# Score products of 8 to 136 columns run on to 192 and 256 columns in a two-attention kernel

## The chip, the cores and the metric

One core of one Trainium2 chip runs the whole program. The metric is device time in microseconds (us): the median of repeated executions of a kernel. A separate execution is taken with the hardware profiler; everything that is read below from the page or the trace comes from that one.

## The reference

Two attention layers read inputs of their own, each 2048 positions by 1024 features with 32 heads of 32 features, and their outputs are set side by side:

```python
q, k, v = split(x @ wqkv)                      # both layers, 32 heads of 32
# layer A: query s sees keys s, s-2, ..., s-14 (8 keys, every second one)
# layer B: query s sees keys s-255 ... s
o = softmax(mask(q @ k.T * 32 ** -0.5)) @ v
y = o @ wo
return concatenate([yA, yB], axis=-1)
```

## The kernel before

**Tiling.** The work is cut into eight units of 512 positions: units 0 to 3 are layer B ("dense": each 128 queries meet up to 384 keys), units 4 to 7 are layer A ("window"). For layer A even and odd positions are first parted on the host, so that eight neighbouring keys are seen; each 128 queries then meet 136 keys. A unit that has keys ahead of its first position reads them as a halo (`has_halo`). Every unit has eight groups of four heads.

**Stages of a group.** Q and K are made by 48 TensorE products of 512 columns (line 418), written out in two parts, and stacked by DMA into the tiles `qst` (128 by 4 heads by 512) and `kst` (128 by 4 heads by 768), two buffers each. Then come two passes over the scores:

- The *first pass* (`first`, line 714) has a block of 128 queries as the stationary operand and n keys as the moving one; 16 products a group, n being 136 (window), 384 (dense), or 128 and 256 where a unit has no halo. VectorE masks each and takes the maximum (line 719), ScalarE takes the exponential and its sum (line 724). The 16 sums give one row of numbers for each head, which VectorE writes into rows 96 to 127 of `qst` (lines 753 and 759), head after head.
- The *second pass* (`second`, line 599 in `window`, line 799 in the dense case) has 128 keys as the stationary operand and n queries as the moving one, so that its result comes out transposed and already normalized after one exponential (lines 606 and 806). Here n is 8, 136 or 128 in the window units, and 128, 256 or 384 in the dense ones; two or four heads (`pack`) share a PSUM bank `ps`, at columns `i * n`. Masks follow on VectorE or GpSimd (lines 616, 612, 785, 788), and products with V (lines 640 and 846).

All scores are products of `fp32r` tiles, one matmul and one weight load each. The products with V read plain `f32` tiles and take two matmuls each. V itself is made on line 481 (256 or 512 columns), the output product is line 543 (512 columns); weights and x are split in two parts by VectorE (lines 164 and 172). Line 138 issues the loads of the weights.

**Order.** One loop writes the program out, with a model of the engines' times (`Clock`). It holds four lists: `aux` (line 753), second-pass items with the V products, first-pass items, and the big products of 512 or 256 columns. At each step it takes the item that the model says can begin first, so products of few columns stand between big ones. An item's cost in the model is a number given by hand. Scores go through a ring of four PSUM banks (`rs`, `NS` = 4), and a bank is taken again when ScalarE's exponential has read it.

Of the kernel before, what the change touches and what calls it, by code (L numbers as in the profile page):

```python
# [14 lines left out]
P = 128  # L15
# [14 lines left out]
NX, NST, NN = 9, 1, 3  # L30
TAIL, XAT = 4, 1
C1, C3, CG, CV = 0.108, 0.2, 0.231, 0.242
TERMS = ((0, 0), (0, 1), (1, 0))


# [146 lines left out]
def kernel(ctx, tc, xs, wqk, wv, wo, outs, units):  # L182


    nc = tc.nc
    U = len(units)
    ctx.enter_context(tc.manual_schedule())
    const = ctx.enter_context(tc.tile_pool(name="const", bufs=1))
    raws = ctx.enter_context(tc.tile_pool(name="raws", bufs=NRAW))
# [41 lines left out]
    for p in plan:  # L231
# [3 lines left out]
        elif p[0] == "v":  # L235
            s0, n = VPARTS[p[2]]
# [102 lines left out]
    def qk_items(u, s):  # L339
# [58 lines left out]
        for t in range(2):  # L398
# [14 lines left out]
            def run(k, t=t, h=h):  # L413
                if k == 0:
                    h["ps"], h["b"] = rg.take()
                    h["w"], _ = st.get(where["qk", u, s, t])
                for i, (a, b) in enumerate(TERMS):
                    nc.tensor.matmul(h["ps"], h["w"][:, a, k * P:(k + 1) * P], xt[u][k][:, b, :],  # L418
# [101 lines left out]
    def o_items(u, n):  # L520
        h = {}

        last = u == U - 1
        ring = rs if last and n == 3 else rg

        def ready(k):
            if (u * NG + k) not in done["ot"]:
                return None
            if k == 0:
                st.split_to(where["o", u, n] + 1)  # L530
                r = st.ready[where["o", u, n]]
                h["r"] = r if isinstance(r, list) else [r, r]
                return latest(ring.when(), h["r"][0], done["ot"][u * NG])
            return max(done["ot"][u * NG + k], h["r"][k // 4])

        def run(k):
            if k == 0:
                h["ps"], h["b"] = ring.take()
                w, _ = st.get(where["o", u, n])
                h["w"] = [(w[i // 4], i % 4 * P) if isinstance(w, list) else (w, i * P) for i in range(NK)]  # L540
            w, c = h["w"][k]
            for i, (a, b) in enumerate(TERMS):
                nc.tensor.matmul(h["ps"], w[:, a, c:c + P], ot[u, k][:, b, :],  # L543
                                 start=(k == 0 and i == 0), stop=(k == NK - 1 and i == 2))
            if k == 3 and (not last or n == 0 or n > 2):
                st.split_to(where["o", u, n] + (3 if last and n == 0 else 2))
            if k == 5 and last and n in (1, 2):
                st.split_to(where["o", u, n] + 3)

        def after(k):  # L550
            if k == NK - 1:
                done["out"][u, n] = True
                for f in list(stores.values()):
                    f()
                o = pbuf[:, n % 4, :S] if last else stp.tile([P, S], F32, tag="ost", name="ost")
                e = copy_out(o, h["ps"], h["b"], ring)

                def store():
                    if stores.pop((u, n), None):
                        nc.scalar.dma_start(outs[u, n], o)  # L560
                        ck.load("store", e)

                stores[u, n] = store
                ck.defer(e, store)

        return [(lambda k=k: ready(k), lambda k=k: run(k), 3 * CG, lambda k=k: after(k)) for k in range(NK)]

    def x_items(u):
        xt[u], xready[u] = [], []

        def run(g):
            a, b = st.get(where["x", u, g])
            xt[u] += a
            xready[u] += b

        return [[(lambda: 0.0, lambda g=g: run(g), 0.0, lambda: None)] for g in range(4)]


    def window(u, s, h):
        has_halo = units[u][3]  # L580
        buf = s % 2
        hg = u * NG + s
        q, kk = qst[buf], kst[buf]
        vp, vc = vpart[s]
        v = vbuf[vp]
        two = []
        kbs = [(-1, 0, 8, 4)] if has_halo else []
        kbs += [(0, 0, 136, 2), (1, 128, 136, 2), (2, 256, 136, 2), (3, 384, 128, 4)]
        nk = len(kbs)
        at = [sum(k[2] for k in kbs[:i]) for i in range(nk)]  # L590

        def second(ki, hp):
            kb, q0, n, pack = kbs[ki]
            if hp == 0:
                h["left", ki] = 4 // pack
            ps, bank = rs.take()
            for i in range(pack):
                j = hp * pack + i
                nc.tensor.matmul(ps[:, i * n:(i + 1) * n], kk[:, j, 256 + kb * P:256 + (kb + 1) * P],  # L599
                                 q[:, j, q0:q0 + n], start=True, stop=True)  # L600
            w = pbuf[:, hp * pack:hp * pack + pack, at[ki]:at[ki] + n]
            if ki == nk - 1 and hp == 4 // pack - 1:
                free_keys(hg)

            def expo():
                nc.scalar.activation(w, ps[:, :pack * n].rearrange("p (j n) -> p j n", j=pack), AF.Exp)
                e = ck.use("act", pack * n / 1200 + 0.055, ck.now, pfree[0])
                rs.give(bank, e)

                def masks():  # L610
                    if kb < 0:
                        nc.gpsimd.affine_select(w, w, pattern=[[0, pack], [-1, n]], compare_op=ALU.is_ge, fill=0.0,
                                                base=-121, channel_multiplier=1)
                        r = ck.use("pool", 0.21, e)
                    else:
                        nc.vector.tensor_tensor(w, w, cst["keep_w"][:, None, :n].to_broadcast([P, pack, n]),  # L616
                                                op=ALU.min)
                        r = ck.use("dve", pack * n / 960 + 0.07, e, port=True)
                    h["left", ki] -= 1
                    h["pr", ki] = max(h.get(("pr", ki), 0.0), r)  # L620

                ck.defer(e - 0.1, masks)

            return expo

        def values_ready(ks):
            if ks[-1] == nk - 1 and hg >= NO and ((hg - NO) // NG, NG - 1) not in done["out"]:
                return None
            if (u, vp) not in done["v"] or any(h.get(("left", k), 1) for k in ks):
                return None  # L630
            return latest(done["v"][u, vp], ro.when() if ks[0] == 0 else 0.0, *[h["pr", k] for k in ks])

        def values(ks):
            for ki in ks:
                kb, q0, n, pack = kbs[ki]
                if ki == 0:
                    h["o"], _ = ro.take()
                slot = (4 * u + kb) % 6
                for j in range(4):
                    nc.tensor.matmul(h["o"][32 * j:32 * j + 32, q0:q0 + n],  # L640
                                     v[:, slot, vc + 32 * j:vc + 32 * j + 32], pbuf[:, j, at[ki]:at[ki] + n],
                                     start=(ki == 0), stop=(ki == nk - 1), skip_group_check=True)

            def after():
                pfree[0] = ck.now
                finish(u, s, h)

            return after

        def seconds(ki):  # L650
            pack = kbs[ki][3]
            for hp in range(4 // pack):
                two.append(Item(lambda hp=hp: latest(rs.when(), h["rows"] and h["rows"][hp * pack + pack - 1]),
                                lambda ki=ki, hp=hp: second(ki, hp), pack * C1))

        for ki in range(nk):
            seconds(ki)
        ks = tuple(range(nk))
        two.append(Item(lambda: values_ready(ks), lambda: values(ks), C3 + sum(max(0.05, kbs[k][2] / 592) for k in ks)))
        return two  # L660
# [28 lines left out]
    def attention(u, s):  # L689
# [3 lines left out]
        q, kk = qst[buf], kst[buf]  # L693
# [5 lines left out]
        def first(b, j):  # L699
# [6 lines left out]
            else:  # L706
                full, mask = 136, cst["mask_w"]
                cut = 8 if (b == 0 and not has_halo) else 0
            n = full - cut
            c1 = 256 + P * b + P  # L710
            c0 = c1 - n
            i = j * 4 + b
            ps, bank = rs.take()
            nc.tensor.matmul(ps[:, :n], q[0:96, j, b * P:(b + 1) * P], kk[0:96, j, c0:c1],  # L714
                             start=True, stop=True)
            nm, sm = h["nm"][:, i:i + 1], h["sm"][:, i:i + 1]

            def top():
# [72 lines left out]
        def second(ki, hp):  # L791
            kb, q0, n, pack = kbs[ki]
# [3 lines left out]
                h["left", ki, pr] = 2 // pack  # L796
            ps, bank = rs.take()
            for i, j in enumerate(heads):
                nc.tensor.matmul(ps[:, i * n:(i + 1) * n], kk[:, j, 256 + kb * P:256 + (kb + 1) * P],  # L799
                                 q[:, j, q0:q0 + n], start=True, stop=True)  # L800
            w = pbuf[:, heads[0]:heads[0] + pack, at[ki]:at[ki] + n]
            if ki == nk - 1 and hp == 4 // pack - 1:
                free_keys(hg)
# [66 lines left out]
    for u in range(U):  # L870
        for s in range(NG):
            a, b = attention(u, s)
# [21 lines left out]
    n = TAIL  # L894
# [84 lines left out]
```

## Time and profile before

| | |
|---|---|
| median of 3 runs | 1926.64 us (1926.56 to 1929.82) |
| profiled execution: its time, its span | 1927.66 us, 1926.0 us |
| TensorE matmul (PE) busy | 1897.7 us, 99% of the span |
| weight loads (PEld) busy | 1565.1 us, 81% |
| VectorE (DVE), ScalarE (ACT), GpSimd (POOL) busy | 74%, 50%, 20% |
| mean granted TensorE clock | 0.997 |
| products of line 714 / 599 / 799 | 1024 / 576 / 704 |

PE is matmul work, PEld the loads of the stationary operand. A group row of the profile gives the line, the operation, the tiles written and read, rows times columns of the stationary operand, the moving operand and the count, then busy time, the mean duration of one in ns, and the engine's idle time ahead of them with what ended it. A duration holds the way through the array, so that durations of neighbours overlap; what a product costs a busy TensorE is read from the times at which stretches of products begin.

### The profile page before, as it was taken

The page shows a single profiled execution, that of the slowest core. Times are in us where ns is not written, and L with a number is a line of the kernel's source. Part 1 is how long each engine was busy: PE and PEld are TensorE (multiplying, and loading weights), DVE is VectorE, ACT ScalarE, POOL GpSimd, SP SyncE. Part 2 cuts the span into 40 slices and gives each one's busy share as a digit, 9 for nine tenths or more (in the row PEclk, how much of TensorE's full clock was granted, in tenths as well). Part 3 has the DMA queues.
Part 4 walks back from the last instruction along what each step waited for, and adds up shares of the span by engine and source line. Part 5 has one row for each costly group of instructions (what it writes and reads, how often), then busy time and mean ns, then how long its engine had stood idle before and what let it go on. Part 6 is the DMA issues. An engine that isn't in the chain of part 4 may idle for free. (4 is left out here: it accounts for less than half of the span.)

```text
span 1926.0 us, 34516 instructions
## 1 busy us (share of the span) xinstructions
PE 1897.7 (99%) x11840; PEld 1565.1 (81%) x11840; DVE 1430.3 (74%) x3989; ACT 965.1 (50%) x3139; POOL 385.7 (20%) x926
## 2 busy tenths in 40 slices
PE   8999999999999999999999999999999999999999
PEld 6887687888778887788877888888888888888887
DVE  6777767669777688777787778866796768867673
ACT  3565665655665656664565434533444444534451
POOL 2223432323221322222322001100010000100000
PEclk9999999999999999999999999999999999999999
DMA  6555545455545455545464556456564655555451
GB/s 191 153 143 159 164 146 167 138 152 174 156 144 171 121 164 152 156 143 151 132 165 129 163 171 193 131 167 180 141 184 141 176 163 176 153 167 167 128 149 66
DMA packets 135727, 297.96 MB, mean 155 GB/s; under 512 B 14464, under 2 KB 40064, under 8 KB 135552
## 3 DMA queue, kind: packets, MB, share of 16 engines
q1 hardware_dynamic: 83456, 123.77, 26.1%
q0 software_dynamic: 41472, 151.01, 23.7%
q10 hardware_dynamic: 10624, 20.98, 3.0%
q8 instruction: 94, 1.54, 0.4%
q14 instruction: 81, 0.66, 0.1%
HBM read 167.77 MB, written 27.26 MB: 101 GB/s over the span
## 5 line engine op out<-in xcount | busy, mean ns | idle before, releaser
L418 PE MATMUL g<-x,w 128*128 128x512 f32 x3072 | 798.2, 397 | 8.8 <-DVE w L164 8.2
L418 PEld LDWEIGHTS g<-x,w 128*128 128x128 f32 x3072 | 555.5, 189 | 106.6 <-DVE w L164 8.6
L724 ACT ACTIVATE s<-s,nm 128x384 f32<-128x384 f32 (+3 forms) x1024 | 452.7, 443 | 224.1 <-DVE nm L719 214.6
L481 PE MATMUL g<-w,x 128*128 128x256 f32 (+1 forms) x2304 | 404.6, 322 | 0.9 <-DVE w L172 0.7
L543 PE MATMUL g<-ot,w 128*128 128x512 f32 x1416 | 356.8, 398 | 0.0
L481 PEld LDWEIGHTS g<-w,x 128*128 128x128 f32 x2304 | 332.5, 190 | 26.6 <-DVE w L172 2.5
L172 DVE TENSOR_TENSOR w<-raw,w 128x512 fp32r<-128x512 f32 x518 | 339.7, 697 | 8.9
L719 DVE CUSTOM_DVE_ANT_0 s<-s,mask_d 128x384 f32<-128x384 f32 (+2 forms) x512 | 263.0, 554 | 93.4 <-PE s L714 92.3
L543 PEld LDWEIGHTS g<-ot,w 128*128 128x128 f32 x1416 | 259.6, 190 | 50.8 <-issue 1.0
L785 POOL TENSOR_SCALAR_AFFINE_SELECT pbuf<-pbuf 128x128 f32<-128x128 f32 (+1 forms) x600 | 213.8, 384 | 313.0 <-ACT pbuf L806 303.0
L806 ACT ACTIVATE pbuf<-s 128x384 f32<-128x384 f32 (+2 forms) x480 | 202.8, 503 | 94.2 <-PE s L799 93.3
L714 PE MATMUL s<-kst,qst 96*128 96x384 f32 (+3 forms) x1024 | 238.0, 302 | 5.6 <-ACT s L724 4.4
L714 PEld LDWEIGHTS s<-kst,qst 96*128 96x128 f32 x1024 | 182.5, 189 | 51.8 <-ACT s L724 10.8
L719 DVE CUSTOM_DVE_ANT_0 s<-s,mask_w 128x136 f32<-128x136 f32 (+1 forms) x512 | 141.9, 323 | 103.4 <-PE s L714 102.4
L724 ACT ACTIVATION_READ_ACCUMULATOR s<-s,nm 128x1 f32 x1024 | 210.4, 206 | 0.0
L355 ACT ACTIVATE nat<-g 128x512 fp32r<-128x512 f32 x128 | 76.6, 599 | 240.2 <-PE g L418 225.6
L759 DVE TENSOR_TENSOR qst<-s,pick 32x512 fp32r<-32x512 f32 x256 | 158.4, 675 | 37.9 <-PE s L753 37.0
L164 DVE CAST w<-raw 128x1024 fp32r<-128x1024 f32 x259 | 179.3, 692 | 7.0 <-DMA raw<-wv 4.0
L359 DVE SCALAR_TENSOR_TENSOR nat<-g,nat 128x512 fp32r<-128x512 f32 x128 | 88.3, 690 | 116.1 <-ACT nat L355 115.5
L138 POOL DMA_DIRECT2D raw<-wqk x126 | 68.7, 545 | 496.6 <-DVE w L172 234.7
L799 PEld LDWEIGHTS s<-qst,kst 128*128 128x128 f32 x704 | 112.8, 189 | 42.6 <-ACT s L724 14.9
L719 DVE DVE_READ_ACCUMULATOR2_ANT nm<- 128x1 f32 x1024 | 144.4, 141 | 0.5
(55 smaller groups left out, 1184.8 us busy)
## 6 DMA issues: line engine op xcount, KB each, us to landing
raw<-wqk POOLq DMA_DIRECT2D x126, 512.0 KB, 3.9
qst<-nat SPq DMA_DIRECT2D x192, 256.0 KB, 3.8
kst<-nat SPq DMA_DIRECT2D x192, 256.0 KB, 4.0
raw<-wv POOLq DMA_DIRECT2D x70, 512.0 KB, 4.4
raw<-wo POOLq DMA_DIRECT2D x64, 512.0 KB, 4.0
raw<-xs POOLq DMA_DIRECT2D x28, 512.0 KB, 4.6
outs<-ost ACTq DMA_DIRECT2D x56, 256.0 KB, 2.6
halo<-nat SPq DMA_DIRECT2D x40, 256.0 KB, 4.4
```

The lines of the kernel that those rows point to most:

```text
L164: nc.vector.tensor_copy(t[:, 0, :], raw)
L172: nc.vector.tensor_tensor(o, a, b, op=ALU.subtract)
L418: nc.tensor.matmul(h["ps"], h["w"][:, a, k * P:(k + 1) * P], xt[u][k][:, b, :], start=(k == 0 and i == 0), stop=(k == NK - 1 and i == 2))
L481: nc.tensor.matmul(ps, xt[u][kw * g + k][:, a, p0:p0 + P], h["w"][g][:, c, k], start=(first and t == 0 and half == 0), stop=(last and t == 2),
L543: nc.tensor.matmul(h["ps"], w[:, a, c:c + P], ot[u, k][:, b, :], start=(k == 0 and i == 0), stop=(k == NK - 1 and i == 2))
L714: nc.tensor.matmul(ps[:, :n], q[0:96, j, b * P:(b + 1) * P], kk[0:96, j, c0:c1], start=True, stop=True)
L719: nc.vector.tensor_tensor_reduce(ps[:, :n], ps[:, :n], mask[:, cut:full], scale=-1.0, scalar=BIG, op0=ALU.add, op1=ALU.min, accum_out=nm)
L724: nc.scalar.activation(ps[:, :n], ps[:, :n], AF.Exp, bias=nm, scale=-1.0, accum_out=sm)
L759: nc.vector.tensor_tensor(q[96:P, j, :].rearrange("p (b s) -> p b s", s=P), ps[0:32, None, 0:P].to_broadcast([32, 4, P]), cst["pick"][0:32 ...
L785: nc.gpsimd.affine_select(w, w, pattern=[[0, m], [step, n]], compare_op=ALU.is_ge, fill=0.0, base=base, channel_multiplier=chan)
L799: nc.tensor.matmul(ps[:, i * n:(i + 1) * n], kk[:, j, 256 + kb * P:256 + (kb + 1) * P], q[:, j, q0:q0 + n], start=True, stop=True)
L806: nc.scalar.activation(w, ps[:, :pack * n].rearrange("p (j n) -> p j n", j=pack), AF.Exp)
```

## The change

A helper `wide` widens the products of the second pass: up to 256 moving columns, as far as the bank (`512 - c`) and the four heads' queries (`2048 - 512 * j - q0`) go. The added columns are the queries that follow in `qst`, which can be the next head's. They land in PSUM columns that the next head's product of the same bank overwrites, or that nobody reads. First-pass products are widened to 192 keys: for the first block of queries to the right, for the others to the left, and VectorE and ScalarE then read the n columns that count. Products that already have as many columns stay as they are. `ORDER` is the order 0 to 7 that the units had. The costs in the ordering model are not changed, nor is any operation on another engine.

By the loops, 544 first-pass products go to 192 columns (448 from 136, 96 from 128). Of the second pass, 736 go to 256 columns: 384 from 136, 288 from 128 and 64 from 8; 64 products of 128 columns stay, since the fourth head has no columns behind it.

```diff
+ORDER = (0, 1, 2, 3, 4, 5, 6, 7)
+WIDE1, WIDE2 = 192, 256
...
+    units, xs = [units[i] for i in ORDER], [xs[i] for i in ORDER]
...
-                        nc.scalar.dma_start(outs[u, n], o)
+                        nc.scalar.dma_start(outs[ORDER[u], n], o)
...
+    def wide(ps, c, n, keys, q, j, q0):
+        x = max(n, min(WIDE2, 512 - c, 2048 - 512 * j - q0))
+        nc.tensor.matmul(ps[:, c:c + x], keys, q.rearrange("p j s -> p (j s)")[:, 512 * j + q0:512 * j + q0 + x],
+                         start=True, stop=True)
...
 # second, in window and in the dense case
-                nc.tensor.matmul(ps[:, i * n:(i + 1) * n], kk[:, j, 256 + kb * P:256 + (kb + 1) * P],
-                                 q[:, j, q0:q0 + n], start=True, stop=True)
+                wide(ps, i * n, n, kk[:, j, 256 + kb * P:256 + (kb + 1) * P], q, j, q0)
...
 # first
-            nc.tensor.matmul(ps[:, :n], q[0:96, j, b * P:(b + 1) * P], kk[0:96, j, c0:c1],
-                             start=True, stop=True)
+            x = max(n, WIDE1)
+            if b == 0:
+                nc.tensor.matmul(ps[:, :x], q[0:96, j, :P], kk[0:96, j, c0:c0 + x], start=True, stop=True)
+            else:
+                nc.tensor.matmul(ps[:, :x], q[0:96, j, b * P:(b + 1) * P], kk[0:96, j, c1 - x:c1], start=True, stop=True)
+                ps = ps[:, x - n:]
```

More of the change, by code (lines that the diff above doesn't have):

```diff
@@ L798, in second @@
             for i, j in enumerate(heads):
-                nc.tensor.matmul(ps[:, i * n:(i + 1) * n], kk[:, j, 256 + kb * P:256 + (kb + 1) * P],
-                                 q[:, j, q0:q0 + n], start=True, stop=True)
+                wide(ps, i * n, n, kk[:, j, 256 + kb * P:256 + (kb + 1) * P], q, j, q0)
             w = pbuf[:, heads[0]:heads[0] + pack, at[ki]:at[ki] + n]
```

## The prediction

> **What bounds the kernel now.** I read the page's busy line first, then the groups kept apart by shape, then the timeline of TensorE around products of few columns, and last the windows of the tail.
>
> ```profile
> PE 1897.7 (99%) x11840; PEld 1565.1 (81%) x11840; DVE 1430.3 (74%) x3989; ACT 965.1 (50%) x3139; POOL 385.7 (20%) x926
> ```
>
> TensorE is busy for 1897.7 of 1926.0 us. Whatever a product costs more there goes to the end, unless it falls ahead of a place where TensorE would have waited anyway. So the question is what a product of few columns costs now, and what one of 192 or 256 costs. The groups give counts and durations:
>
> ```profile
> L714 PE MATMUL s<-kst,qst 96*128 96x136 f32 x448 | 83.1, 261 | 4.1 <-ACT s L724 3.9
> L714 PE MATMUL s<-kst,qst 96*128 96x256 f32 x32 | 7.8, 304 | 0.0
> L599 PE MATMUL s<-qst,kst 128*128 128x136 f32 x384 | 53.5, 273 | 0.1
> L599 PE MATMUL s<-qst,kst 128*128 128x8 f32 x64 | 8.3, 235 | 0.0
> L799 PE MATMUL s<-qst,kst 128*128 128x256 f32 x224 | 41.0, 289 | 0.2 <-ACT s L724 0.2
> L799 PE MATMUL s<-qst,kst 128*128 128x128 f32 x224 | 35.8, 258 | 2.0 <-ACT s L724 1.8 <-DVE qst L759 0.2
> ```
>
> Durations overlap, so they are no price on a full engine. The price is in the timeline (first column the start, second the length, last the count): the time from one stretch's start to the next one's, shared among its products.
>
> ```profile
> 1242.25 2.69 PE L418 MATMUL g<-x,w 128*128 128x512 f32 x11
> 1244.77 1.72 PE L599 MATMUL s<-qst,kst 128*128 128x8 f32 x14
> 1246.32 0.90 PE L418 MATMUL g<-x,w 128*128 128x512 f32 x3
> ...
> 1865.49 0.90 PE L543 MATMUL g<-ot,w 128*128 128x512 f32 x3
> 1866.23 1.27 PE L599 MATMUL s<-qst,kst 128*128 128x136 f32 x10
> 1867.33 0.90 PE L543 MATMUL g<-ot,w 128*128 128x512 f32 x3
> 1868.08 0.56 PE L599 MATMUL s<-qst,kst 128*128 128x128 f32 x4
> 1868.47 0.50 PE L714 MATMUL s<-kst,qst 96*128 96x136 f32 x3
> 1868.81 0.91 PE L543 MATMUL g<-ot,w 128*128 128x512 f32 x3
> ...
> 399.76 3.04 PE L481 MATMUL g<-w,x 128*128 128x256 f32 x24
> 402.64 0.33 PE L799 MATMUL s<-qst,kst 128*128 128x128 f32 x2
> ...
> 285.04 0.86 PE L418 MATMUL g<-x,w 128*128 128x512 f32 x3
> 285.74 0.64 PE L799 MATMUL s<-qst,kst 128*128 128x256 f32 x4
> 286.21 1.55 PE L418 MATMUL g<-x,w 128*128 128x512 f32 x6
> ```
>
> - 512 columns: 11 products from 1242.25 to 1244.77, 0.229 us each; I use 0.23.
> - 136 columns: from 1865.49 to 1867.33 lie three of 512 and ten of 136; (1.84 - 0.69) / 10 = 0.115 us.
> - 128 columns, and first-pass ones of 136: from 1867.33 to 1868.81 lie three of 512, four of 128 and three of 136; (1.48 - 0.69) / 7 = 0.113 us. I take 0.112 for 128.
> - 8 columns: the stretch at 1244.77 holds ten of 136 and four of 8 (the row names its first shape); 1.55 / 14 = 0.111 us.
> - 256 columns: 24 from 399.76 to 402.64, 0.120 us each; from 285.04 to 286.21 three of 512 and four of 256: (1.17 - 0.69) / 4 = 0.120 us.
>
> The reader is to see that 8, 128 and 136 columns cost the same 0.111 to 0.115 us. Something other than columns sets that price; each product has one load of 128 stationary columns, and I take that load to be it. From 256 to 512 columns the price rises by 0.11 us, 0.43 ns a column; back from 256 on that slope, columns set the price only above some 240.
>
> **The change part by part.** Nothing is removed. No instruction, wait, transfer or order changes as written; what changes is the length of 1280 products.
>
> *First pass, 544 products to 192 columns.* By the slope 192 columns take 120 - 64 x 0.43 = 92 ns, under the 111 to 115 ns that the load takes. Price: 0 on a full TensorE, hidden by the loads. If that cover is gone, because the engine stands free when the product comes, its end counts: on the durations of 96 rows (261 at 136, 304 at 256) 192 columns end some 20 ns later, 544 x 20 = 10.9 us if all of them counted. A gain has no row to come from: the loads remain. I take 0, since TensorE is 99% busy.
>
> *Second pass, 736 products to 256 columns.* 384 x (120 - 115) = 1.9 us; 288 x (120 - 112) = 2.3 us; 64 x (120 - 111) = 0.6 us; together 4.8 us, all on TensorE. From below: if 256 columns cost no more than the floor of 112 ns, 0 for those of 128 and 384 x 3 = 1.2 us gained on those of 136, so -1 us. From above, by the ends of products (289 ns against 273, 258 and 235): 384 x 16 + 288 x 31 + 64 x 54 = 18.5 us. I take 4.8: the row of 24 in a stretch is the nearest to a full engine.
>
> *What swallows some of it.* The list of TensorE's waits has ten of up to 1.6 us on VectorE or ScalarE (five of line 714 for line 724, five of line 753 for line 745). Products added shortly before such a place run while VectorE works on. With 20 us ahead of each of ten places, 200 of 1926 us, a tenth is swallowed: an estimate, 0.5 us.
>
> *New reads.* A widened product of the last key block reads up to 128 columns of the next head, whose rows 96 to 127 are written by line 759. In the window units its four heads share one bank and wait for all four writes already; in the dense ones this block is in the last lot, long after. No wait, price 0. Line 719 and line 724 read at an offset of 56 or 64 columns, the same number of columns; 0.
>
> *Sum* against the profiled execution: 1927.66 + 4.8 - 0.5 = 1931.96 us. That execution stands 1.02 us over the median, so the median goes to 1930.9 us, 0.22% more.
>
> **The rivals.**
>
> *The tail keeps its clock.* The windows of the tail (columns: busy time and count of PE, PEld, DVE, ACT, POOL, then the granted clock) show the one place where the clock falls, and the timeline shows its price:
>
> ```profile
> 1870.00:1872.00 2.00, 0.61 (x2) 0.47 (x2) 2.00 (x12) 1.15 (x6) 0.00 (x0) 0.91 0.67 225
> 1872.00:1874.00 2.00, 2.00 (x41) 1.50 (x41) 0.60 (x6) 0.03 (x1) 0.00 (x0) 0.50 0.06 23
> ```
>
> ```profile
> 1872.13 2.12 PE L640 MATMUL o<-pbuf,vbuf 128*32 128x8 f32 x40
> ...
> 1875.96 6.41 PE L543 MATMUL g<-ot,w 128*128 128x512 f32 x15
> ...
> 1882.26 3.65 PE L543 MATMUL g<-ot,w 128*128 128x512 f32 x15
> ...
> 1891.02 1.19 PE L640 MATMUL o<-pbuf,vbuf 128*32 128x8 f32 x40
> ```
>
> After a stretch of few-column products and a wait of 1.59 us the clock is at 0.50; fifteen products of 512 take 6.41 us, the next fifteen 3.65 at full clock, 2.8 us more; the forty of line 640 take 2.12 against 1.19 us, 0.9 more, which the wait behind them may hide. Wider products keep TensorE at work for more of that stretch, and everything ahead has moved by some microseconds. If the clock does not fall, 2.8 to 3.7 us come back: 1930.9 - 3.7 to 1930.9 - 2.8, 1927.2 to 1928.1, no slower than before by what a measurement tells. For it: the fall follows the least busy stretch. Against: the other waits of up to 1.6 us in that list did not lower the clock, so the fall hangs on more than the wait, and seven products of 120 or 56 more columns add only tenths of a microsecond of work. The Trainium skill's page "TensorE: Matmul & The Clock Gate", Part 1, says that the clock follows activity in free-running windows of 3413 ns, which makes it a matter of phase as well; the fall in this trace, at 0.50, agrees with its two states.
>
> *Faster: both that and a free second pass.* If 256 columns in short runs hide the load altogether, at 112 ns, the sum is -1 instead of 4.8, and with the kept clock 1926.6 - 1 - 2.8 to 3.7 gives 1921.9 to 1922.8. It decides where 256 columns cost under 115 ns. Against it: no stretch of 256 here comes under 0.119.
>
> *Late ends.* VectorE waited 186 times for a product of line 714. If each of these 20 ns came onto the path, 3.7 us more: 1934.6. Against it: VectorE is busy 74% and not the bound.
>
> *Columns cost in full.* If each added column costs its 0.43 ns, 98,816 in the second pass and 31,232 in the first make 55.9 us: 1982. Against it: 8 columns cost as much as 136. The same page's section "Back-to-back issue gap" gives N / 2.4 + 2.5 ns for a warm product; by it the 130,048 added columns would be an estimate of 54 us, and the same two rows speak against it.
>
> **How the numbers follow.** My forecast has 0.55, the kept clock 0.20, faster 0.16, late ends 0.07, full columns 0.02. A measurement of this kernel tells about 0.2% from no change, 3.9 us: the bounds are 1922.8 and 1930.5. The forecast lies 0.4 us above the upper one; with prices of 118 to 123 ns its own range is 1929 to 1933, of which I put 0.36 above and 0.19 within. The kept clock is within (0.18) or, with cheap products, faster (0.02). Faster gives 0.15 and 0.01. So faster 0.17, same 0.38, slower 0.45. The range goes from 1923.5 to 1935.0: it holds the forecast, the kept clock and late ends, and leaves out most of the faster case and full columns, 0.17.
>
> **What would show it.** In the changed trace, stretches of ten or fourteen second-pass products should take 0.120 us each and first-pass pairs the same as now; PE busy should grow by about 4 us, mostly after 1030 us, where the window units are. DVE, ACT and POOL times stay. The prediction is wrong if first-pass products cost more than 0.115, if stretches of 256 take 0.112 or less, or if the clock windows of the tail hold 1.00 or new falls show elsewhere.

## The result and the profile after

Over 20 executions each, the median goes from 1926.97 to 1929.10 us; the ratio is 1.0013, with a 95% interval of 1.0007 to 1.0019: some 2.5 us slower. That is the direction of the forecast at about half of its size, and inside the 0.2% that the prediction called "same": an outcome that it gave 0.38, against 0.45 for a slower one.

The profiled execution of the changed kernel took 1928.07 us with a span of 1926.2 us, only 0.2 us over the span before. That it is so little has two halves. The first is the price of the columns. In the timeline of TensorE around the stretches shown of before (start, length, count last; lines 418, 481, 543, 599 and 714 are now 421, 484, 546, 585 and 727):

```profile
1245.97 1.87 PE L585 MATMUL s<-qst,kst 128*128 128x256 f32 x14
1247.68 0.61 PE L421 MATMUL g<-x,w 128*128 128x512 f32 x2
...
1866.08 0.37 PE L727 MATMUL s<-kst,qst 96*128 96x192 f32 x2
1866.29 0.90 PE L484 MATMUL g<-w,x 128*128 128x256 f32 x6
1867.02 2.24 PE L546 MATMUL g<-ot,w 128*128 128x512 f32 x9
1869.09 0.88 PE L585 MATMUL s<-qst,kst 128*128 128x256 f32 x6
1869.81 0.86 PE L546 MATMUL g<-ot,w 128*128 128x512 f32 x3
1870.51 1.39 PE L585 MATMUL s<-qst,kst 128*128 128x256 f32 x10
1871.74 0.86 PE L546 MATMUL g<-ot,w 128*128 128x512 f32 x3
```

The stretch of fourteen that took 1.55 us takes 1247.68 - 1245.97 = 1.71 us, 0.122 each. Three of 512 and ten of the second pass took 1.84 us and take 1871.74 - 1869.81 = 1.93, so (1.93 - 0.69) / 10 = 0.124 each against 0.115. The pair of first-pass products and the six of line 484 behind it take 0.94 us. The same eight products before:

```profile
1861.87 0.34 PE L714 MATMUL s<-kst,qst 96*128 96x136 f32 x2
1862.04 0.92 PE L481 MATMUL g<-w,x 128*128 128x256 f32 x6
1862.80 2.23 PE L543 MATMUL g<-ot,w 128*128 128x512 f32 x9
```

They took 1862.80 - 1861.87 = 0.93 us: 192 keys cost nothing that shows. The two kernels issue the same 11840 matmuls, so starts can be compared: the stretch of fourteen begins 1.20 us later than before (1245.97 against 1244.77), the nine of line 546 begin 4.22 us later (1867.02 against 1862.80). Some 0.5 us of that is one wait ahead of first-pass products ("0.54 <-issue" in the row at 1266.81). The profile does not show what it waits for; such a wait of 0.3 to 0.9 us stands in five of the six profiles with a widened first pass and in none of the six others.

The second half is the tail. From those nine products to the end of the span the kernel before took 1926.0 - 1862.8 = 63.2 us, the changed one 1926.2 - 1867.0 = 59.2. The windows show why (busy time and count of PE, PEld, DVE, ACT, POOL, then the granted clock):

```profile
1874.00:1876.00 2.00, 0.67 (x4) 0.32 (x2) 2.00 (x10) 1.01 (x6) 0.00 (x0) 1.00 0.78 219
1876.00:1878.00 2.00, 1.62 (x42) 1.15 (x42) 1.15 (x9) 0.77 (x4) 0.00 (x0) 1.00 0.15 57
```

The wait for ScalarE is still there (0.67 us of work in 2 us), but this time the clock stays at 1.00. The prediction names such a tail among the signs of its being wrong. The other engines' times stay, as it said; but busy time says little of TensorE. The page's first row has PE at

```profile
PE 1898.1 (99%) x11840; PEld 1567.6 (81%) x11840; DVE 1430.7 (74%) x3989; ACT 964.1 (50%) x3139; POOL 383.1 (20%) x926
```

0.4 us more than before and not the 4 us expected: the halved clock had stretched products in the kernel before. Its fifteen products of 512 columns behind the waits took 6.41 us; in the changed kernel they take 3.62.

### The profile page after: what moved, and what is told of

Read it like the earlier page. It is cut to its first block, busy times and chain, and to the rows that moved or that the text cites. A ratio compares the mean times of both kernels' runs of the same rounds, so it can differ in the third digit from the quotient of the medians.

```text
span 1926.2 us, 34617 instructions
## 1 busy us (share of the span) xinstructions
PE 1898.1 (99%) x11840; PEld 1567.6 (81%) x11840; DVE 1430.7 (74%) x3989; ACT 964.1 (50%) x3139; POOL 383.1 (20%) x926
## 4 chain that ended last, share of the span: by engine, by line
PE 94%; DVE 3%; ACT 1%; DMA 1%; issue 1%; POOL 0%; ACTq 0%; DVEq 0%
PE g L421 36%; PE g L546 18%; PE g L484 17%; PE s L585 9%; PE s L727 6%; PE o L858 4%; PE s L725 2%; PE o L649 2%; ACT s L737 1%; DVE w L174 1%; DVE qst L772 1%; DMA raw<-xs 0%; DVE s L732 0%; DVE x L174 0%; DVE w L166 0%
## 5 line engine op out<-in xcount | busy, mean ns | idle before, releaser
L546 PE MATMUL g<-ot,w 128*128 128x512 f32 x1416 | 351.6, 393 | 0.0
L585 PEld LDWEIGHTS s<-qst,kst 128*128 128x128 f32 x1280 | 193.2, 189 | 49.7 <-ACT s L737 14.6
L585 PE MATMUL s<-qst,kst 128*128 128x256 f32 (+2 forms) x1280 | 221.5, 296 | 3.9 <-ACT s L737 2.6
L727 PE MATMUL s<-kst,qst 96*128 96x192 f32 (+2 forms) x768 | 192.4, 311 | 4.5 <-ACT s L737 4.2
L727 PEld LDWEIGHTS s<-kst,qst 96*128 96x128 f32 x768 | 139.4, 189 | 42.8 <-ACT s L737 10.8
```

What stands on the lines that cost most here:

```text
L585: nc.tensor.matmul(ps[:, c:c + x], keys, q.rearrange("p j s -> p (j s)")[:, 512 * j + q0:512 * j + q0 + x], start=True, stop=True)
L727: nc.tensor.matmul(ps[:, :x], q[0:96, j, b * P:(b + 1) * P], kk[0:96, j, c1 - x:c1], start=True, stop=True)
```

## The experiments

Times are medians; "before" is the kernel before, in the experiments run on the same chip among them. The clock is the mean over a kernel's executions, each of which has its own mean granted clock.

| kernel | us | before | ratio (95%) | clock |
|---|---|---|---|---|
| the change | 1929.10 | 1926.97 | 1.0013 (1.0007 to 1.0019) | 0.9985 |
| 1 second pass alone | 1930.97 | 1927.59 | 1.0021 (1.0012 to 1.0030) | 0.9979 |
| 2 first pass alone | 1926.40 | 1927.59 | 0.9992 (0.9983 to 1.0000) | 0.9978 |
| 3 both at 192 | 1926.47 | 1927.59 | 0.9996 (0.9987 to 1.0005) | 0.9981 |
| 4 first pass at 256 | 1930.49 | 1927.59 | 1.0015 (1.0007 to 1.0024) | 0.9980 |
| 5 before, waits filled | 1925.14 | 1927.50 | 0.9984 (0.9975 to 0.9993) | 0.9997 |
| 6 first pass, waits filled | 1924.34 | 1927.50 | 0.9981 (0.9972 to 0.9990) | 0.9994 |
| 9 the change, waits filled | 1929.40 | 1927.02 | 1.0009 (1.0000 to 1.0018) | 0.9995 |
| 10 as 5, beside 9 | 1925.47 | 1927.02 | 0.9993 (0.9984 to 1.0002) | 0.9993 |

The kernel before had a mean clock of 0.9973 (33 executions, beside 1 to 4), 0.9974 (21, beside 5 to 8) and 0.9977 (21, beside 9 and 10). For its 20 executions beside the change the clock is not on record.

**1. The second pass alone.**

```diff
-WIDE1, WIDE2 = 192, 256
+WIDE1, WIDE2 = 0, 256
```

> The change's second pass alone: 736 products at 256 columns, the first pass as before. Theory 1 (each product pays the larger of a floor of 0.112 to 0.115 us, taken to be its weight load, and its columns; 256 columns are 0.120): stretches of ten cost 1.20 us against 1.15, and before any wait the sum is +4.8 us, the same as for the whole change; time +2 to +4.5 us by how often the clock falls in the tail. Rival (late ends of the first pass are what costs): within 1 us of before.

It costs 3.4 us by the medians and 4.0 by the ratio: the change's whole price lies here, as theory 1 has it. Late ends of the first pass are not what costs.

The two profiles show the price without the falls of the clock. Both programs issue the same products in the same order, and from 402.64 us (a row shown in the prediction) to the nine products at 1862.80 the kernel before has a clock of 1.00 throughout. The same two places in this kernel, again with a clock of 1.00 between them, are:

```profile
403.34 0.40 PE L585 MATMUL s<-qst,kst 128*128 128x256 f32 x2
...
1867.51 2.23 PE L546 MATMUL g<-ot,w 128*128 128x512 f32 x9
```

That is 1464.17 us against 1460.16: 4.0 us more for the 646 widened products that lie between, 6.2 ns each, or 4.6 us for all 736.

**2. The first pass alone.**

```diff
-WIDE1, WIDE2 = 192, 256
+WIDE1, WIDE2 = 192, 0
```

> The change's first pass alone: 544 products at 192 columns, the second pass as before. Theory 1: 192 columns (0.092 us by the slope) stay under the floor, a pair costs 0.228 us as before, time 0 +- 1 us. Rival (late ends): each product ends some 20 ns later, up to +3.7 us. If the clock in the tail is what the wider products help, this one should keep it about as often as the whole change, since half of the products near the tail's wait are of the first pass.

The ratio's interval ends at 1.0000: no cost, perhaps a gain of a microsecond. Between the two places used above, with 503 widened products, its profile takes 1863.82 - 403.80 = 1460.02 us against 1460.16. That agrees with theory 1 and rules out 3.7 us of late ends. The clock expectation fell: its mean of 0.9978 is over the 0.9973 of before but under the change's 0.9985.

**3. Both passes at 192.**

```diff
-WIDE1, WIDE2 = 192, 256
+WIDE1, WIDE2 = 192, 192
```

> Both passes at 192 columns instead of 192 and 256. Theory 1: 192 columns stay under the floor in the second pass too, so a stretch of ten costs 1.15 us as before and the time is 0 +- 1 us against before, some 3 us under the whole change. Rival (columns cost in full, 0.43 ns each): second pass 384 x 56 + 288 x 64 + 64 x 184 columns = 51,712, +22 us.

The time is that of before within its interval, and 4.5 us under experiment 1: the step lies between 192 and 256 columns. In the timeline three of 512 and ten of 192 take 1867.76 - 1865.89 = 1.87 us, 0.118 each, between 0.115 and 0.124:

```profile
1865.89 0.88 PE L546 MATMUL g<-ot,w 128*128 128x512 f32 x3
1866.61 1.32 PE L585 MATMUL s<-qst,kst 128*128 128x192 f32 x10
1867.76 0.89 PE L546 MATMUL g<-ot,w 128*128 128x512 f32 x3
```

So the floor is nearly but not wholly flat in stretches of ten; the full price of columns would have been 22 us.

**4. The first pass at 256.**

```diff
-WIDE1, WIDE2 = 192, 256
+WIDE1, WIDE2 = 256, 0
```

> First pass at 256 columns instead of 192, the second pass as before. Theory 1: 544 x (0.120 - 0.113) = +3.8 us on TensorE, where 192 columns cost nothing: the step lies between 192 and 256. Rival (all of the floor is something else than 111 ns of load and 256 columns fit under it when 96 rows are read): 0 +- 1 us.

It is 2.9 us slower than before and 4.1 slower than experiment 2, which differs only in 256 for 192: 4.1 / 544 = 7.5 ns a product. The step at 256 columns shows in both passes. The rival falls.

**5. The kernel before with the tail's waits filled.** The extra products write bank columns that nobody reads.

```diff
+            for _ in range({10: 7, 13: 5}.get(4 * b + j, 0) if hg == U * NG - 1 else 0):
+                nc.tensor.matmul(ps[:, 136:512], q[0:96, j, b * P:(b + 1) * P], kk[0:96, j, 256:632], start=True, stop=True)
```

> The kernel before, with seven and five extra products of 376 columns issued in the last group after the first-pass products behind which TensorE waits 1.59 and 1.15 us in the tail; they write bank columns that nobody reads. Activity theory (the clock falls because the stretch around these waits is too empty): at 0.175 us each the waits are filled, the tail keeps its clock in nearly all runs, the mean granted clock rises from 0.9973 to 0.999 or more, and the median falls by 2 to 3 us against before. Phase theory (it falls or not by where a window begins, whatever the load): clock and time as before, or up to 0.5 us more.

The two waits stand in the profile of the kernel before as

```profile
1871.37 0.83 PE L714 MATMUL s<-kst,qst 96*128 96x136 f32 x2 [1.59 <-ACT s L724]
...
1875.33 0.83 PE L714 MATMUL s<-kst,qst 96*128 96x136 f32 x2 [0.66 <-ACT s L724]
```

The second is 0.66 us long; the 1.15 us of the expectation is the time from the start of the product ahead of it (1874.18) to this one.

With the fill the clock is 0.9997, eight of eleven executions show 1.000, and the time falls by 2.4 us. The timeline and the windows of the tail:

```profile
1869.46 1.42 PE L717 MATMUL s<-kst,qst 96*128 96x376 f32 x7
1871.21 0.69 PE L714 MATMUL s<-kst,qst 96*128 96x136 f32 x2 [0.33 <-ACT s L726]
1871.82 1.18 PE L640 MATMUL o<-pbuf,vbuf 128*32 128x8 f32 x40
1872.94 0.33 PE L714 MATMUL s<-kst,qst 96*128 96x136 f32 x1
1873.10 1.08 PE L717 MATMUL s<-kst,qst 96*128 96x376 f32 x5
```

```profile
1870.00:1872.00 2.00, 1.64 (x20) 1.11 (x22) 2.00 (x11) 1.18 (x6) 0.00 (x0) 1.00 0.55 217
1872.00:1874.00 2.00, 2.00 (x46) 1.66 (x36) 0.44 (x4) 0.93 (x4) 0.00 (x0) 1.00 0.03 10
```

The first wait shrinks from 1.59 to 0.33 us, the second is gone, and forty products of line 640 take 1.18 us instead of 2.12. Nothing ahead of the tail was touched, so the phase theory falls in its form "whatever the load": where that stretch is full enough, the clock stays. None of the four profiles of filled kernels (5, 6, 9 and 10) has a fall there, and five of the eight others do (before and experiments 1 to 4). Why the remaining three keep their clock with the waits unfilled, no run shows.

**6. The free first pass with the waits filled.**

```diff
-WIDE1, WIDE2 = 192, 256
+WIDE1, WIDE2 = 192, 0
...
+                for _ in range({10: 7, 13: 5}.get(4 * b + j, 0) if hg == U * NG - 1 else 0):
+                    nc.tensor.matmul(ps[:, 192:512], q[0:96, j, b * P:(b + 1) * P], kk[0:96, j, 256:576], start=True, stop=True)
```

> First pass at 192 columns, second pass as before, and the two waits of the tail filled with seven and five extra products of 320 columns. Activity theory: the clock is kept at least as often as with the filled kernel before, and the free first pass costs nothing: 2 to 4 us under before, the fastest of all. Phase theory: as the first pass alone, -1 us +- 1.

This is the fastest kernel of all, 3.2 us under before by the medians. Whether the first pass adds to experiment 5 can't be told: their intervals overlap. Its profile shows the other place where the clock falls, which the fill leaves alone, at about 200 us; seven of the twelve profiles have it, that of the kernel before has not. The same fall, in the profile of experiment 2:

```profile
201.00:203.00 2.00, 2.00 (x6) 1.63 (x6) 1.30 (x4) 0.64 (x3) 2.00 (x6) 0.50 0.03 8
203.00:205.00 2.00, 2.00 (x8) 1.83 (x8) 1.37 (x5) 1.64 (x4) 0.82 (x3) 0.68 0.53 147
```

**7. A half load by itself.**

```diff
+                if n <= 136:
+                    nc.tensor.matmul(ps[:64, i * n:i * n + 8], kk[:, j, 256 + kb * P:256 + kb * P + 64],
+                                     q[:, j, q0:q0 + 8], start=True, stop=True)
```

> The kernel before, with one more product of 8 columns and 64 stationary columns ahead of each of the 800 second-pass products of at most 136 columns; the real product overwrites it. Theory 1 in its form 'the floor is the load of 128 stationary columns': a half load takes some 0.056 us, so 800 x 0.056 = +45 us. Rival (the floor belongs to each product, whatever it loads): 800 x 0.112 = +90 us.

One execution took 1976.89 us, 49.4 over before: 49.4 / 800 = 0.062 us each. In the timeline fourteen pairs stand between the first and the last of these rows (the rows between have the same two lines in turn):

```profile
1483.79 0.17 PE L600 MATMUL s<-qst,kst 128*64 128x8 f32 x1
1483.82 0.25 PE L602 MATMUL s<-qst,kst 128*128 128x8 f32 x1
...
1486.23 0.90 PE L481 MATMUL g<-w,x 128*128 128x512 f32 x3
```

2.44 / 14 = 0.174 us a pair, 0.06 over a product alone. A product with half of the stationary columns costs about half of the floor, with the same 8 moving columns. Nor is 0.06 us what it takes to issue any product: the forty products of line 640 in the timeline of experiment 5, with 32 stationary columns, take 1872.94 - 1871.82 = 1.12 us, 0.028 each. So the floor is not a fixed cost of each product; it goes with the stationary columns, as their load would.

**8. The second pass up to 384 columns.**

```diff
-WIDE1, WIDE2 = 192, 256
+WIDE1, WIDE2 = 0, 384
```

> Second pass widened up to 384 columns where the bank and the four heads have them, the first pass as before. Theory 1 (above some 240 columns each column costs 0.43 ns): a product of 384 columns costs 0.175 us, 0.06 more than the floor. By the bank most pairs go to 384 and 376 columns, quartets of 128 to 384, 384, 256 and 128: about 600 products x 0.06 = +35 us. Rival (full price from the first column): the 256-column version's +4 us would have been +40, so this one would show +90.

One execution took 1969.47 us, 42 over before. The count of the expectation was off: products of 256 columns that lead a bank grew too, so that the profile has

```profile
L585 PE MATMUL s<-qst,kst 128*128 128x384 f32 x880 | 241.7, 345 | 3.5 <-ACT s L737 2.1 <-ACT pbuf L818 1.0 <-DVE qst L772 0.2
L585 PE MATMUL s<-qst,kst 128*128 128x376 f32 x160 | 53.3, 333 | 0.0
```

880, of which 256 had 384 columns before and 112 come from 256. With 0.061, 0.058 and 0.055 us more, 512, 160 and 112 products make 31.2 + 9.3 + 6.2 = 46.7 us. That is 5 us over the 42 measured; that this one execution kept its clock (0.999 against a mean of 0.9974 before) may hide some 2 of them (an estimate at the rate of experiment 5, where 0.0023 of the clock were worth 2.4 us), and the rest is open. A stretch of fourteen gives the price:

```profile
1480.88 2.61 PE L585 MATMUL s<-qst,kst 128*128 128x384 f32 x14
1483.33 0.85 PE L484 MATMUL g<-w,x 128*128 128x512 f32 x3
```

2.45 / 14 = 0.175 us, 0.055 over 256 columns: above the floor each column is paid for.

**9 and 10. The change with the waits filled, beside the filled kernel before.** Number 9 is experiment 6 with `WIDE2` at 256, number 10 is experiment 5 again.

> The whole change with the two waits of the tail filled by seven and five extra products of 320 columns. If the change's time is +4.3 us of second-pass columns less some 2 us of kept clock, then with the clock kept in both kernels the full price shows: +4 to +5 us over the filled kernel before on the same chip, mean clock 0.999 or more in both. Rival (the second pass costs only the 2 us that the first comparison showed, and the clock is chance): +2 us over it.

> The filled kernel before on the same chip as the filled change, for that comparison: 2 to 3 us under the kernel before, mean clock 0.999 or more.

With the clock at 0.9995 and 0.9993 the change costs 1929.40 - 1925.47 = 3.9 us. So that is its price once the clock is out of it, just under the band expected and good to about a microsecond (each kernel's eleven executions spread over 3 to 4 us), and the rival's 2 us falls. Number 10 was only 1.6 us under before, and its interval takes in no change; before itself had a better clock in that set (0.9977).

## Why the prediction was right, and where it was not

*The floor.* That products of 8 to 136 columns all pay the same and that this is the load of 128 stationary columns was read from stretches; experiment 7 shows that it goes with the stationary columns (0.062 us for half of them) and experiments 3, 4 and 8 show that columns take over between 192 and 256.

*First pass, 0.* Right: experiment 2 costs nothing, and eight products in the timeline take 0.94 us against 0.93. Late ends (the rival at 3.7 us) did not come. The new reads cost nothing either: TensorE waits once, for 0.2 us, on the writes of line 759, as before.

*Second pass, 4.8 us, less 0.5 swallowed.* Right: 4.6 us by the start times of experiment 1 (6.2 ns a product against 4.8 / 736 = 6.5), 4.0 by its ratio, and 3.9 between experiments 9 and 10 against a net 4.3. In the two stretches shown, of ten and fourteen, the price was 0.122 to 0.124 us, 9 to 11 ns over before; such a stretch alone would have made the sum too large. That a tenth is swallowed was not tested by itself.

*The tail's clock.* This is the step that failed: it stood as a rival of all or nothing at 0.20, while it belonged in the sum as a mean. The clock falls in some executions and not in others. In the sets that record it the kernel before had a mean clock of 0.9973 to 0.9977, and the change 0.9985: by 1926 x 0.0008 to 0.0012 the change loses 1.5 to 2.3 us less of TensorE's clock. A microsecond of clock is worth less than a microsecond of time, since TensorE waits during part of a fall: in experiment 5, 1926 x 0.0023 = 4.4 us of clock were worth 2.4 us. At that rate 0.8 to 1.3 us come back on average, an estimate, and the price of 3.9 becomes 2.6 to 3.1 us, against 2.1 by the medians and 2.5 by the ratio. With that term the forecast would have stood at about 1930 us, within 0.2%, and not 0.4 us above that bound. So of the some 2 us by which the forecast was too high, the clock explains about half, a price of 3.9 for 4.3 another 0.4, and the rest is no more than the medians can tell.

*Its cause.* Filling the waits shows that a stretch that is full enough keeps the clock. That the widened products keep the clock for the same reason is argued, not shown by itself: all four partial versions (experiments 1 to 4) had a mean clock of 0.9978 to 0.9981, over before's 0.9973 on the same chip, yet none reached the change's 0.9985, and the first pass alone still fell for 6.8 us in its profile. Experiments 1 and 2 also add up to the change without a clock of its own: 3.4 - 1.2 = 2.2 us by the medians. In the changed kernel's profile the first wait is 1.33 us and the clock stays; in those of experiments 1 to 4 it is 1.40 to 1.49 us and the clock falls, but that is one execution of each. Whether 0.9985 is more than the chance of one set, and how full a stretch has to be, stays open.

*Columns in full, and the faster case.* 55.9 us did not come; experiment 3 shows that 192 columns hide under the load, all but 0.003 us in a stretch of ten. The faster case needed 256 columns at the floor, and the stretches of ten and fourteen took 0.122 to 0.124 us.

## What to carry to other kernels

Read the price of a short product from the time between the starts of stretches on a full engine, not from its duration: here all widths up to about 192 cost nearly one weight load, and between there and 256 columns begin to be paid for. Where two programs issue the same products in the same order, compare the start of the same product in both traces: that gave the price of the change free of the clock, while single executions spread over 5 us and more. Look through the windows for places where the granted clock falls, and count such a fall as a term that comes in a part of the executions; on an engine that is 99% busy, twelve useless products in two waits were worth 2 us, as much as the whole change took.

## What the runs showed of the hardware

- In the kernel before, a wait of 1.59 us behind short products was followed by half clock during 10.2 us; in other profiles such falls lasted 3.4 or 6.8 us, so that the lengths seen are once, twice and three times 3.4 us. Seven products in the first wait and five in the second, about 2 us of work, kept it away.
- The same kernel's executions differ by several microseconds with this clock: of 75 executions of the kernel before, the eleven with a mean clock of 0.999 had a median of 1925.4 us, the eleven with 0.996 one of 1930.6 us.
- On a full TensorE a product with 128 stationary and 8 to 136 moving columns took 0.111 to 0.115 us, one with 64 stationary and 8 moving columns some 0.06 (experiment 7).
